# Reordering the first FFN group of a fused mLSTM and squared-ReLU FFN kernel on all its engine queues

## The chip, the cores and the metric

The kernel runs on one core of a Trainium2 chip. A core has five engines that work side by side, each with its own queue that is worked off strictly in the order of the program: TensorE (PE, the matmuls, with the loads of its weights shown as PEld), VectorE (DVE), ScalarE (ACT), GpSimd (POOL) and SyncE (SP), which here issues nearly all DMAs. Matmuls write to PSUM banks; the other data lies in SBUF. An instruction that needs another engine's result waits for a semaphore, and everything behind it on its own queue waits with it. The metric is the time of one execution on the device in microseconds (us), lower is better.

## The reference

The first part is an mLSTM cell over 4 batches, 8 heads, 768 time steps and heads of 40 columns, as a recurrence:

```python
for t in range(S):
    m_new = np.maximum(f_gate[:, :, t] + m, i_gate[:, :, t])
    f_stab = np.exp(f_gate[:, :, t] + m - m_new)
    i_stab = np.exp(i_gate[:, :, t] - m_new)
    m = m_new
    C = f_stab[:, :, None, None] * C + i_stab[:, :, None, None] * np.einsum('bhd,bhe->bhde', vt, kt)
    n = f_stab[:, :, None] * n + i_stab[:, :, None] * kt
    h_tilde = np.einsum('bhde,bhe->bhd', C, qt)
    nq = np.einsum('bhd,bhd->bh', n, qt)[:, :, None]
    denom = np.maximum(np.abs(nq), 1.0)
    o = 1.0 / (1.0 + np.exp(-o_gate[:, :, t]))
    y[:, :, t] = o * h_tilde / denom
```

Its output, as a matrix x of 3072 tokens by 320 columns, goes through an FFN with w_in (320 x 2048) and w_out (2048 x 320), whose values arrive as 64-bit floats:

```python
h = np.maximum(x @ w_in, 0.0)
return (h * h @ w_out).astype(np.float32)
```

## The kernel before, in words

The recurrence is computed by chunks of 128 tokens. There are 24 chunks, six to a batch; a chunk is called s. For each chunk these steps are written, each of them a small function:

- `load(s)`, `load_A(s)`, `load_o(s)` fetch k, q and v, the row of decays spread over the partitions, and the output gate. All are issued by SP.
- `weigh(s)`: POOL masks the decays (affine_select, L312), ACT makes the weights W from them (eight exponentials, L318), POOL multiplies v by the weights of the last row (vw, L329).
- `transposes(s)`: PE transposes k and q (L342); the copies out of PSUM are kT on ACT and qT on DVE (L346).
- `scores(s)`: PE multiplies qT and kT (L355). `weighted(s)`: DVE multiplies the scores by W into P_sb (L365).
- `attend(s)`: PE makes hi (the carried state times q, L376), dC (the state's increment, L383) and hp (P_sb times v, L390). DVE scales and adds them (num, L396 and L412; C_sb, L401), POOL updates the state (L404, L409), and DVE divides by the denominator and multiplies by the gate (dm and x_sb, L414 to L421). POOL copies the last 64 columns of x a second time (L422), so that PE can use both halves of its rows.
- `turn_rows(s)`: PE transposes x (L431), ACT copies it into xT (L432).

The FFN works on groups of four chunks (512 tokens). `ffn1` takes a pair of 128-column blocks of the hidden layer: six matmuls into two PSUM banks (L446, L451), the rectifier on ACT (r_sb, L454) and the square on DVE (g, L455). `ffn2` multiplies g by w_out (L493) in two parts for each chunk, and ACT copies the result out (L499). The first group is different: its chunks come out while it runs, so it is computed in two halves of 256 tokens with four units each by `ffn1_half` (L470, L477; rectifier L485, square L486). These eight units are called u0 to u7 here: u = 4 * half + the loop's own u.

The weights arrive as 64-bit floats and are rounded to 32 bits on the chip, in 26 pieces: ten of w_in (512 columns wide) and then sixteen of w_out (320 wide). One `rounding.step()` does one piece: two ACT operations of the piece after it (`words`, L179 and L181), three DVE operations (`join`, L190, L194, L195), one POOL add that writes the weights (L199), and a DMA that fetches the raw words of the fourth piece after it (L170). The pools bound how far these run ahead: four raw buffers, two of mag and low.

The order on every queue is written out by hand (`manual_schedule`): engines do not reorder, so the order of the statements is the order of the work. PSUM has eight banks: three for the attention ("at"), three for h_ps, two for o_ps; a pool hands its banks out in turn, and a writer waits until the readers of the tile that had the bank are done. `idle(n)` is n matmuls of zeros.

Before the loop over u, chunks 0 and 1 go through all their steps and chunk 2 through its transposes. Then a unit with an even u does score(s), turn_rows(s - 1), its rounding steps, ffn1_half, and the weights of chunk s + 1; one with an odd u does attend(s), its rounding steps, ffn1_half and transposes(s + 1). The number of rounding steps in u0 to u7 is 2, 3, 2, 4, 4, 4, 4 and 0. After the loop the general schedule runs four units of FFN to one chunk.

Of the kernel before, what the change touches and what calls it, by code (L numbers as in the profile page):

```python
# [9 lines left out]
F32 = mybir.dt.float32  # L10
# [19 lines left out]
def kernel(  # L30
# [326 lines left out]
                )  # L357
        d["sc"] = sc

    def weighted(s):  # L360
        d = st[s]
        sc = d["sc"]
        d["P"] = work.tile([P, 2, PR, P], F32, name="P_sb", bufs=1)
        for i in range(2):
            nc.vector.tensor_tensor(  # L365
                d["P"][:, i], sc[i], d["W"][:].rearrange("p (j two) t -> p j two t", two=2)[:, :, i, :], op=ALU.mult,
            )

    def attend(s):
        b, c = divmod(s, NB)  # L370
        d = st[s]
        C = st.get("C")
        if c > 0:
            hi = ps_at.tile([P, H, D1], F32, name="hi", tag="at")
            for j in range(PR):
                nc.tensor.matmul(  # L376
                    hi[:, 2 * j : 2 * j + 2, :].rearrange("p h d -> p (h d)"), lhsT=d["qT"][:, j, :],
                    rhs=C[:, j].rearrange("p h d -> p (h d)"), start=True, stop=True,
                )
        if c + 1 < NB:  # L380
            dC = ps_at.tile([P, PR, 2, D1], F32, name="dC", tag="at")
            for j in range(PR):
                nc.tensor.matmul(  # L383
                    dC[:, j].rearrange("p h d -> p (h d)"),
                    lhsT=d["kq"][:, 0, 2 * j : 2 * j + 2, :].rearrange("p h d -> p (h d)"),
                    rhs=d["vw"][:, 2 * j : 2 * j + 2, :].rearrange("p h d -> p (h d)"), start=True, stop=True,
                )
        hp = ps_at.tile([P, H, D1], F32, name="hp", tag="at")
        for h in range(H):
            nc.tensor.matmul(  # L390
                hp[:, h, :], lhsT=d["P"][:, h % 2, h // 2, :], rhs=d["va"][:, h, :], start=True, stop=True,
            )
        num = hp
        if c > 0:
            num = work.tile([P, H, D1], F32, name="num")
            nc.vector.tensor_tensor(  # L396
                num[:], hi[:], eA_T[:, b, c, :].unsqueeze(2).to_broadcast([P, H, D1]), op=ALU.mult,
            )
        if c + 1 < NB:
            Cn = work.tile([P, PR, 2, D1], F32, name="C_sb")  # L400
            nc.vector.tensor_tensor(Cn[:], dC[:], bdm[:], op=ALU.mult)  # L401
            if c > 0:
                Cd = work.tile([P, H, D1], F32, name="Cd")
                nc.gpsimd.tensor_tensor(  # L404
                    Cd[:], C[:].rearrange("p j i d -> p (j i) d"),
                    d["dec"][:].unsqueeze(2).to_broadcast([P, H, D1]), op=ALU.mult,
                )
                Cf = Cn[:].rearrange("p j i d -> p (j i) d")
                nc.gpsimd.tensor_tensor(Cf, Cf, Cd[:], op=ALU.add)  # L409
            st["C"] = Cn  # L410
        if c > 0:
            nc.vector.tensor_tensor(num[:], num[:], hp[:], op=ALU.add)  # L412
        dm = work.tile([P, H], F32, name="dm")
        nc.vector.tensor_scalar(dm[:], num[:, :, D], scalar1=-1.0, scalar2=1.0, op0=ALU.mult, op1=ALU.max)  # L414
        nc.vector.tensor_tensor(dm[:], dm[:], num[:, :, D], op=ALU.max)
        nc.vector.reciprocal(dm[:], dm[:])

        x = d["x"] = work.tile([P, 3 * P], F32, name="x_sb")
        x3 = x[:, :DM].rearrange("p (h d) -> p h d", d=D)
        nc.vector.tensor_tensor(x3, num[:, :, :D], d["og"], op=ALU.mult)  # L420
        nc.vector.tensor_tensor(x3, x3, dm[:].unsqueeze(2).to_broadcast([P, H, D]), op=ALU.mult)  # L421
        nc.gpsimd.tensor_copy(x[:, DM:], x[:, DM - KR : DM])  # L422

    def turn_rows(s):
        d = st[s]
# [31 lines left out]
    def ffn1_half(g, half, pp):  # L457
# [16 lines left out]
        for n in range(2):  # L474
            for i in range(2):
# [2 lines left out]
                    hs[i][:, n, :], lhsT=w_in2[rows, 2 * pp + n, :], rhs=xT[rows, 2, cols],  # L478
                    start=False, stop=(n == 1),
                )  # L480
        g4 = st["g2"][:, 4 * pp : 4 * pp + 4, cols].rearrange("p (n two) t -> p n two t", two=2)
        for i in range(2):
            r = ffn.tile([P, W], F32, name="r_sb", bufs=4)
            r2 = r[:].rearrange("p (n t) -> p n t", n=2)
            nc.scalar.activation(r2, hs[i][:], AF.Relu)  # L485
            nc.vector.tensor_tensor(g4[:, :, i, :], r2, r2, op=ALU.mult)  # L486

    def ffn2(g, j, part):
        if part == 0:
# [26 lines left out]
    def attend_on(s):  # L516
        do(attend, s)
        do(load, s + 4)
        if 4 <= s < 8:
            load_o(2 * s)  # L520
            load_o(2 * s + 1)
        elif 8 <= s < 16:
            load_o(s + 8)
# [72 lines left out]


    for half in range(2):
        for u in range(4):
            s = 2 * (half + 1) + u // 2  # L600
            if u % 2 == 0:
                score(s)
                if half or u:
                    turn_rows(s - 1)
            else:
                if u == 1:
                    for r in range(s, s + 2 + 2 * half):
                        sigmoid(r)
                attend_on(s)
            for _ in range(IN_DONE[min(u + 1, 3)] - rounding.done if half == 0 and u < 3 else 4):  # L610
                rounding.step()
            if half == 0 and u < 2:
                load(4 + u)
            ffn1_half(0, half, u)
            if u % 2 == 0:
                weigh_on(s + 1)
            else:
                transposes(s + 1)
            if half == 0:
                load_o(4 + u)  # L620
    assert rounding.done == len(pieces)
    turn_rows(5)


# [2 lines left out]
    for n in range(NPAIR, NU * NG):  # L627
        g, u = divmod(n, NU)
        s, at = GT + n // 4, n % 4
        if at == 0:  # L630
            do(score, s)
        if at == 1:
            attend_on(s)
        if at == 3:
            do(turn_rows, s)
            do(transposes, s + 1)
            if s in (7, 15):
                for r in range(s + 1, s + 9):
# [37 lines left out]
```

## Time and profile before

| | before |
|---|---|
| median of 3 runs (lowest to highest) | 636.58 us (636.46 to 636.78) |
| the profiled execution | 636.74 us |
| its span | 635.0 us |
| PE busy | 598.2 us, 94% of the span |
| DVE busy | 226.9 us, 36% |
| ACT busy | 193.2 us, 30% |
| POOL busy | 100.8 us, 16% |
| mean granted TensorE clock | 0.968 |
| moved by DMA | 42.47 MB, mean 67 GB/s |

The profile is one execution. Its span is the time from the first to the last instruction, which is 1.74 us shorter than the execution. A line of a group names the source line, the engine, the operation, out <- in, the count, the busy time and the mean duration in ns. In the chain of waits each row has a start, a duration and what the end of the program waited for then. The granted clock is the share of full speed at which TensorE was run. Some matmuls appear as two records, so counts of L470 or L493 are twice those in the code.

### The profile page before, as it was taken

To read this page: it belongs to the slowest core of one execution; us is meant where nothing else is said; L and a number is where in the kernel's file an instruction comes from. 1 tells how busy PE (TensorE), PEld (TensorE's weight loads), DVE (VectorE), ACT (ScalarE), POOL (GpSimd) and SP (SyncE) were. 2 spreads that over 40 slices of the span, in tenths; PEclk is the share of its full clock that TensorE was granted. 3 is DMA by queue.
4 is the path that set the end of the run, shared out by engine and by line. 5 is a ranking of instruction groups with operands and counts; after the bars stand their busy time and mean duration, and the time that the engine had idled before them with its cause. 6 is when DMAs were issued, how large, how long until landed. Compare 5 with 4: busy or idle time off the path is not lost.

```text
span 635.0 us, 7569 instructions
## 1 busy us (share of the span) xinstructions
PE 598.2 (94%) x2877; PEld 392.9 (62%) x2877; DVE 226.9 (36%) x444; ACT 193.2 (30%) x476; POOL 100.8 (16%) x137
## 2 busy tenths in 40 slices
PE   9974949599999999999999999999999999999997
PEld 5753837477764557764567764567764567743575
DVE  7657667751213432222431223431223431212200
ACT  4646536342153232123132144232114132012200
POOL 3334324221101201001102101001201110000000
PEclk9978878699999999999999999999999999999999
DMA  9889466455312314313313312313211000000000
GB/s 195 207 184 193 85 150 146 105 86 96 63 54 42 74 34 85 63 45 65 52 33 86 63 43 33 64 42 76 44 45 34 0 1 15 17 10 2 0 22 21
DMA packets 130900, 42.47 MB, mean 67 GB/s; under 512 B 101072, under 2 KB 127696, under 8 KB 130864
## 3 DMA queue, kind: packets, MB, share of 16 engines
q1 hardware_dynamic: 130768, 41.79, 31.6%
q8 instruction: 23, 0.38, 0.2%
q10 hardware_dynamic: 96, 0.20, 0.1%
q14 instruction: 13, 0.11, 0.1%
HBM read 37.95 MB, written 4.03 MB: 66 GB/s over the span
## 4 chain that ended last, share of the span: by engine, by line
PE 87%; DVE 5%; ACT 3%; DMA 2%; issue 1%; POOL 1%; SPq 0%; POOLq 0%; ACTq 0%; DVEq 0%
PE o_ps L493 33%; PE h_ps L446 22%; PE h_ps L451 7%; PE hp L390 6%; PE tp L355 5%; PE h_ps L470 3%; PE tp L342 3%; PE hi L376 3%; PE dC L383 2%; PE tp L431 2%; DMA raw<-in_moe_w_out_dram 1%; DVE mag L194 1%; ACT W_sb L318 1%; DVE g L486 1%; DMA kq<-in_q_dram 1%
## 5 line engine op out<-in xcount | busy, mean ns | idle before, releaser
L493 PE MATMUL o_ps<-w_out,g 128*128 128x320 f32 x768 | 213.8, 435 | 0.0
L493 PEld LDWEIGHTS o_ps<-w_out,g 128*128 128x128 f32 x768 | 143.5, 190 | 57.9 <-issue 0.8
L446 PE MATMUL h_ps<-xT,w_in 128*128 128x512 f32 x320 | 146.9, 602 | 0.0
L455 DVE TENSOR_TENSOR g<-r_sb 128x512 f32<-128x512 f32 x80 | 51.7, 688 | 153.2 <-ACT r_sb L454 153.2
L446 PEld LDWEIGHTS h_ps<-xT,w_in 128*128 128x128 f32 x320 | 57.7, 190 | 69.9 <-issue 65.2
L454 ACT ACTIVATE r_sb<-h_ps 128x512 f32<-128x512 f32 x80 | 43.5, 595 | 162.6 <-PE h_ps L451 162.5
L499 ACT COPY y_sb<-o_ps 128x320 f32<-128x320 f32 x24 | 10.2, 425 | 190.4 <-PE o_ps L493 190.4
L355 PE MATMUL tp<-qT,kT 40*128 40x128 f32 x384 | 30.9, 307 | 30.1 <-DVE qT L346 26.3
L318 ACT ACTIVATE W_sb<-A_bc,b_T 128x128 f32<-128x128 f32 x176 | 53.7, 391 | 5.1 <-POOL A_bc L312 5.1
L355 PEld LDWEIGHTS tp<-qT,kT 40*128 40x128 f32 x384 | 27.2, 210 | 40.1 <-issue 31.4
L365 DVE TENSOR_TENSOR P_sb<-tp,W_sb 128x512 f32<-128x512 f32 x48 | 30.9, 684 | 57.3 <-PE tp L355 57.3
L390 PE MATMUL hp<-va,P_sb 128*128 128x41 f32 x384 | 46.1, 280 | 0.0
L451 PE MATMUL h_ps<-xT,w_in 64*128 64x512 f32 x160 | 45.2, 641 | 0.0
L390 PEld LDWEIGHTS hp<-va,P_sb 128*128 128x128 f32 x384 | 44.9, 192 | 0.1
L346 DVE COPY qT<-tp 128x512 f32<-128x512 f32 x23 | 15.8, 687 | 73.6 <-PE tp L342 73.6
L470 PE MATMUL h_ps<-xT,w_in 128*128 128x256 f32 x128 | 36.8, 451 | 0.6 <-ACT xT L432 0.6
L409 POOL TENSOR_TENSOR C_sb<-C_sb,Cd 128x328 f32<-128x328 f32 x16 | 14.0, 876 | 138.8 <-DVE C_sb L401 138.6
L470 PEld LDWEIGHTS h_ps<-xT,w_in 128*128 128x128 f32 x128 | 29.0, 233 | 6.3 <-ACT xT L432 1.0
L329 POOL TENSOR_TENSOR vw<-va,W_sb 128x328 f32<-128x328 f32 x20 | 15.0, 749 | 112.0 <-ACT W_sb L318 107.2
L451 PEld LDWEIGHTS h_ps<-xT,w_in 64*128 64x128 f32 x160 | 12.0, 184 | 30.3 <-issue 30.3
L422 POOL COPY x_sb<-x_sb 128x64 f32<-128x64 f32 x24 | 5.9, 244 | 139.3 <-DVE x_sb L421 139.3
L342 PE MATMUL tp<-ident,kq 128*128 128x128 f32 x192 | 25.4, 274 | 0.2 <-DMA kq<-in_q_dram 0.2
(79 smaller groups left out, 472.1 us busy)
## 6 DMA issues: line engine op xcount, KB each, us to landing
A_bc<-a_rows SPq DMA_DIRECT2D x22, 512.0 KB, 3.8
raw<-in_moe_w_out_dram SPq DMA_DIRECT2D x16, 320.0 KB, 3.4
raw<-in_moe_w_in_dram SPq DMA_DIRECT2D x8, 512.0 KB, 4.9
kq<-in_k_dram SPq DMA_DIRECT2D x24, 160.0 KB, 4.0
kq<-in_q_dram SPq DMA_DIRECT2D x24, 160.0 KB, 4.5
va<-in_v_dram SPq DMA_DIRECT2D x24, 160.0 KB, 4.0
og<-in_o_gate_dram SPq DMA_DIRECT2D x24, 160.0 KB, 4.0
out_dram<-y_sb SPq DMA_DIRECT2D x24, 160.0 KB, 1.8
```

The lines of the kernel that those rows point to most:

```text
L318: nc.scalar.activation(d["W"][:, i * n + h, :], A[i][:, h, :], AF.Exp, bias=b_T[:, b, c, i * n + h : i * n + h + 1],)
L342: nc.tensor.transpose(tp[:, j, :], d["kq"][:, i, 2 * j : 2 * j + 2, :].rearrange("p h d -> p (h d)"), ident[:],)
L355: nc.tensor.matmul(sc[i][:, j, :], lhsT=d["kT"][rows, j, :], rhs=d["qT"][rows, j, :], start=True, stop=True,)
L365: nc.vector.tensor_tensor(d["P"][:, i], sc[i], d["W"][:].rearrange("p (j two) t -> p j two t", two=2)[:, :, i, :], op=ALU.mult,)
L376: nc.tensor.matmul(hi[:, 2 * j : 2 * j + 2, :].rearrange("p h d -> p (h d)"), lhsT=d["qT"][:, j, :], rhs=C[:, j].rearrange("p h d -> p (h ...
L390: nc.tensor.matmul(hp[:, h, :], lhsT=d["P"][:, h % 2, h // 2, :], rhs=d["va"][:, h, :], start=True, stop=True,)
L446: nc.tensor.matmul(h[:], lhsT=w_in[:, a, fb * P : (fb + 1) * P], rhs=xT[:, a, :], start=(a == 0), stop=False,)
L451: nc.tensor.matmul(hs[i][:], lhsT=w_in2[rows, p, :], rhs=xT[rows, 2, :], start=False, stop=True)
L454: nc.scalar.activation(r[:], hs[i][:], AF.Relu)
L455: nc.vector.tensor_tensor(st["g2"][:, 2 * p + i, :], r[:], r[:], op=ALU.mult)
L470: nc.tensor.matmul(hs[i][:, n, :], lhsT=w_in[:, a, fb * P : (fb + 1) * P], rhs=xT[:, a, cols], start=(n == 0 and a == 0), stop=False,)
L493: nc.tensor.matmul(o_ps, lhsT=st["g2"][:, fb, j * P : (j + 1) * P], rhs=w_out[:, fb, :], start=(fb == 0), stop=(fb == NF - 1),)
```

## The change: the same instructions in another order

The computation stays the same, and so does the number of matmuls of the FFN and the attention. What changes:

- `weighted` writes two tiles instead of one with two parts. Chunk 1 takes its two from the pool of r_sb (four buffers), the others from P_sb with two buffers.
- `attend` ends after the matmuls and the state; what makes x of it is a function of its own, `normalise`. The copy of x's last columns moves from POOL to DVE.
- `ffn1_half` issues the matmuls alone. `relu_half` (ACT) and `square_half` (DVE) are called later: the rectifiers of a unit at the start of the next unit, the squares towards that unit's end.
- Ahead of the loop, scores of chunks 0 and 1 are weighted together, two groups of idle matmuls (six and four) go, the rounding steps stand between the attends, and transposes(2) stand between the two remaining groups of idle matmuls.
- In the loop, u0 puts its half unit ahead of scores(2). In odd units the transposes of the next chunk stand ahead of the half unit.
- The rounding steps are spread out: one near the start of each unit and the others at its end, up to the counts in NEXT (6, 8, 10, 12, 15, 18, 21, 24 pieces done after u0 to u7; four are done ahead of the loop). The last two pieces are done after the loop, behind the first W2 unit.
- The fetches of k, q and v of chunks 4 to 9 are spread over the odd units as 4; 5, 6; 7, 8; 9.

```diff
-    def weighted(s):
+    def weighted(s, spare=False):
...
-        d["P"] = work.tile([P, 2, PR, P], F32, name="P_sb", bufs=1)
+        d["P"] = []
         for i in range(2):
+            t = ffn.tile([P, W], F32, name="r_sb", bufs=4) if spare else work.tile([P, W], F32, name="P_sb")
...
-        if c > 0:
-            nc.vector.tensor_tensor(num[:], num[:], hp[:], op=ALU.add)
+
+    def normalise(s):
+        d = st[s]
+        num = d["num"]
+        if num is not d["hp"]:
+            nc.vector.tensor_tensor(num[:], num[:], d["hp"][:], op=ALU.add)
...
-        nc.gpsimd.tensor_copy(x[:, DM:], x[:, DM - KR : DM])
+        nc.vector.tensor_copy(x[:, DM:], x[:, DM - KR : DM])
...
-        g4 = st["g2"][:, 4 * pp : 4 * pp + 4, cols].rearrange("p (n two) t -> p n two t", two=2)
-        for i in range(2):
-            r = ffn.tile([P, W], F32, name="r_sb", bufs=4)
-            r2 = r[:].rearrange("p (n t) -> p n t", n=2)
-            nc.scalar.activation(r2, hs[i][:], AF.Relu)
-            nc.vector.tensor_tensor(g4[:, :, i, :], r2, r2, op=ALU.mult)
+        st["half"] = hs, st["g2"][:, 4 * pp : 4 * pp + 4, cols].rearrange("p (n two) t -> p n two t", two=2)
+
+    def relu_half():
+        if "half" in st:
+            hs, g4 = st.pop("half")
+            rs = []
+            for h in hs:
+                rs.append(ffn.tile([P, 2, W // 2], F32, name="r_sb", bufs=4))
+                nc.scalar.activation(rs[-1][:], h[:], AF.Relu)
+            st["relu"] = rs, g4
+
+    def square_half():
+        if "relu" in st:
+            rs, g4 = st.pop("relu")
+            for i, r in enumerate(rs):
+                nc.vector.tensor_tensor(g4[:, :, i, :], r[:], r[:], op=ALU.mult)
...
     def attend_on(s):
         do(attend, s)
+        do(normalise, s)
...
-    rounding.step()
     weighted(0)
-    idle(6)
+    weighted(1, spare=True)
     load(2)
     load_A(2)
     sigmoid(0)
     sigmoid(1)
     attend(0)
-    weighted(1)
     rounding.step()
+    normalise(0)
     load_o(2)
     load_o(3)
+    attend(1)
+    normalise(1)
+    rounding.step()
     load(3)
     load_A(3)
-    idle(4)
-    attend(1)
     turn_rows(0)
     idle(4)
+    transposes(2)
+    idle(4)
+    turn_rows(1)
+    rounding.step()
     weigh_on(2)
-    transposes(2)
-    turn_rows(1)
-
-
-    for half in range(2):
-        for u in range(4):
-            s = 2 * (half + 1) + u // 2
-            if u % 2 == 0:
-                score(s)
-                if half or u:
-                    turn_rows(s - 1)
+
+
+    NEXT = (6, 8, 10, 12, 15, 18, 21, 24)
+    for u in range(8):
+        s = 2 + u // 2
+        relu_half()
+        if u % 2 == 0:
+            if u == 0:
+                ffn1_half(0, 0, 0)
+                scores(s)
             else:
-                if u == 1:
-                    for r in range(s, s + 2 + 2 * half):
-                        sigmoid(r)
-                attend_on(s)
-            for _ in range(IN_DONE[min(u + 1, 3)] - rounding.done if half == 0 and u < 3 else 4):
-                rounding.step()
-            if half == 0 and u < 2:
-                load(4 + u)
-            ffn1_half(0, half, u)
-            if u % 2 == 0:
-                weigh_on(s + 1)
-            else:
-                transposes(s + 1)
-            if half == 0:
-                load_o(4 + u)
-    assert rounding.done == len(pieces)
+                scores(s)
+                turn_rows(s - 1)
+                ffn1_half(0, u // 4, u % 4)
+            rounding.step()
+            weighted(s)
+            weigh_on(s + 1)
+            square_half()
+        else:
+            if u in (1, 5):
+                for r in range(s, s + 2 + u // 2):
+                    sigmoid(r)
+            attend(s)
+            rounding.step()
+            normalise(s)
+            transposes(s + 1)
+            ffn1_half(0, u // 4, u % 4)
+            square_half()
+            for r in {1: (4,), 3: (5, 6), 5: (7, 8), 7: (9,)}[u]:
+                load(r)
+            if u > 4:
+                load_o(2 * s)
+                load_o(2 * s + 1)
+        while rounding.done < NEXT[u]:
+            rounding.step()
+        if u < 4:
+            load_o(4 + u)
+    relu_half()
+    square_half()
     turn_rows(5)
...
             ffn2(g, *divmod(u - NPAIR, 2))
+        while rounding.done < len(pieces):
+            rounding.step()
         if at == 2:
```

More of the change, by code (lines that the diff above doesn't have):

```diff
@@ L358, in scores @@
         d["sc"] = sc
-    def weighted(s):
+    def weighted(s, spare=False):
         d = st[s]
-        sc = d["sc"]
-        d["P"] = work.tile([P, 2, PR, P], F32, name="P_sb", bufs=1)
+        d["P"] = []
         for i in range(2):
+            t = ffn.tile([P, W], F32, name="r_sb", bufs=4) if spare else work.tile([P, W], F32, name="P_sb")
+            t = t[:].rearrange("p (j t) -> p j t", j=PR)
+            d["P"].append(t)
             nc.vector.tensor_tensor(
-                d["P"][:, i], sc[i], d["W"][:].rearrange("p (j two) t -> p j two t", two=2)[:, :, i, :], op=ALU.mult,
+                t, d["sc"][i], d["W"][:].rearrange("p (j two) t -> p j two t", two=2)[:, :, i, :], op=ALU.mult,
             )
@@ L387, in attend @@
                 )
-        hp = ps_at.tile([P, H, D1], F32, name="hp", tag="at")
+        hp = d["hp"] = ps_at.tile([P, H, D1], F32, name="hp", tag="at")
         for h in range(H):
             nc.tensor.matmul(
-                hp[:, h, :], lhsT=d["P"][:, h % 2, h // 2, :], rhs=d["va"][:, h, :], start=True, stop=True,
+                hp[:, h, :], lhsT=d["P"][h % 2][:, h // 2, :], rhs=d["va"][:, h, :], start=True, stop=True,
             )
-        num = hp
+        d["num"] = hp
         if c > 0:
-            num = work.tile([P, H, D1], F32, name="num")
+            num = d["num"] = work.tile([P, H, D1], F32, name="num")
             nc.vector.tensor_tensor(
```

## The prediction

> **What bounds the kernel now.** I read the granted clock and the busy time by stretch first, then who waits for whom, then the chain of waits through one pair of units. A chunk is 128 tokens (number s); u0 to u7 are the eight half-width units of the first FFN group.
>
> ```profile
> PEclk9978878699999999999999999999999999999999
> ```
> ```profile
> 20.50:138.33 117.83, 85.80 (x521) 70.65 (x520) 79.63 (x148) 60.04 (x136) 43.74 (x49) 0.83 0.66 139
> 63.15:90.30 27.15, 18.35 (x108) 15.27 (x108) 18.54 (x33) 12.26 (x28) 10.04 (x11) 0.81 0.66 139
> 138.33:635.00 496.67, 493.25 (x2240) 310.55 (x2238) 131.52 (x268) 122.63 (x312) 51.14 (x73) 1.00 0.21 43
> ```
> The columns are the stretch, its length, busy PE, PEld, DVE, ACT and POOL, the granted clock, the DMA share and GB/s. From 138.33 us on, PE is busy for 493.25 of 496.67 us at clock 1.00: the change can't shorten that. Before it, from 20.50 to 138.33, PE works 85.80 of 117.83 us, at a mean clock of 0.83. A pair of units (second row) takes 27.15 us.
>
> ```profile
> PE tp L355 <- DVE qT L346: 26.3, 4, 8.8
> ```
> ```profile
> 37.13 2.08 PE L355 MATMUL tp<-qT,kT 40*128 40x128 f32 x16 [3.76 <-ACT kT L346]
> ...
> 137.24 1.16 PE L355 MATMUL tp<-qT,kT 40*128 40x128 f32 x16 [1.35 <-DVE qT L346]
> ```
> The largest wait of PE is the scores waiting for the copy of qT by DVE: 26.3 us in four places. After a pause of 3.76 us the same 16 matmuls take 2.08 us, after 1.35 us 1.16: long pauses also cost clock. The chain through the second of the long pauses shows why the copy is late:
>
> ```profile
> 82.16 4.64 DMA raw<-in_moe_w_out_dram
> ...
> 86.88 0.49 ACT mag L179
> ...
> 87.74 0.49 ACT r_sb L485
> 88.25 1.29 DVE g L486 x2
> 89.55 0.61 DVE qT L346
> ...
> 90.30 2.08 PE tp L355 x16
> ...
> 93.24 0.49 ACT xT L432
> 93.78 6.73 PE h_ps L470 x16
> ```
> A rounding step waits for its raw weights, the rectifiers stand behind it on ACT, the squares behind those on DVE, and the copy of qT behind the squares. PE has nothing in its queue but the scores that need this copy.
>
> **The change, part by part.** First the floor: PE's work from the end of scores(1) to the first W2 matmul, each kind at its full-clock duration.
>
> ```profile
> 6.75 0.86 PE idle L532 x4
> ...
> 19.41 1.09 PE tp L355 x16
> ...
> 21.90 0.85 PE dC L383 x8
> 22.76 1.77 PE hp L390 x16
> ...
> 126.08 1.06 PE h_ps L477 x8
> 127.14 1.05 PE hi L376 x8
> ...
> 129.94 3.53 PE h_ps L470 x16
> ...
> 138.40 4.50 PE o_ps L493 x16
> ...
> 177.50 0.33 PE tp L431 x3
> 177.82 0.87 PE tp L342 x8
> ```
> Scores(1) end at 19.41 + 1.09 = 20.50. Then come attend(0), 0.85 + 1.77 = 2.62; attend(1) to (4), each 1.05 + 0.85 + 1.77 = 3.67, together 14.68; attend(5), which makes no dC, 2.82; five scores, 5.45; eight half units of 3.53 + 1.06 = 4.59, 36.72; five times transposes, 4.35; six turn_rows, 1.98; two idle groups left, 1.72 (the groups of six and four ahead of the attends go). Sum 70.34: the first W2 matmul could start at 90.8 instead of 138.40. So 47.6 us is the most that can be won.
>
> What the edits do to PE's order: transposes(s+1) now stand ahead of a half unit, so 4.59 us of matmuls cover the copies of kT and qT; in u0 the half unit is put ahead of scores(2). The rectifiers move to the start of the next unit and the squares behind the qT copy, so that copy waits for neither. Cover that could fail: three banks hold the half unit's results and two are used per unit, so the second tile of a unit waits for the first rectifier of the unit before, which stands first in ACT's unit. P_sb in separate tiles lets weighted(1) run while attend(0) is still ahead. The copy of x's last 64 columns goes from POOL to DVE: six small instructions, which I put at 0.2 us each (not shown on DVE; between 0 and the 0.49 of the 320-column x operations), and POOL's select and adds no longer wait behind it.
>
> Next the waits that remain. I walked the four in-order queues by hand with these rows:
>
> ```profile
> 66.44 0.42 DVE L190 TENSOR_SCALAR mag<-mag 128x512 f32<-128x512 f32 x1
> 66.89 0.43 DVE L194 TENSOR_SCALAR mag<-mag 128x512 int32<-128x512 int32 x1
> ...
> 67.96 0.42 DVE L190 TENSOR_SCALAR mag<-mag 128x512 f32<-128x512 f32 x1
> 68.42 1.37 DVE L194 TENSOR_SCALAR mag<-mag 128x512 int32<-128x512 int32 x1
> ```
> ```profile
> 36.59 0.74 POOL L329 TENSOR_TENSOR vw<-va,W_sb 128x328 f32<-128x328 f32 x1 [2.56 <-ACT W_sb L318]
> ...
> 68.19 1.31 POOL L199 TENSOR_TENSOR w_in<-mag,low 128x512 int32<-128x512 int32 x1 [6.94 <-DVE mag L195]
> ```
> ```profile
> 34.06 2.44 ACT L318 ACTIVATE W_sb<-A_bc,b_T 128x128 f32<-128x128 f32 x8 [2.49 <-POOL A_bc L312]
> ...
> 50.17 1.28 ACT L275 ACT_TABLE_LOAD   x1
> 51.46 0.83 ACT L275 ACTIVATE og<-og 128x320 f32<-128x320 f32 x2
> ```
> ```profile
> L312 POOL TENSOR_SCALAR_AFFINE_SELECT A_bc<-A_bc 128x1024 f32<-128x1024 f32 x5 | 6.4, 1278 | 0.0
> ```
> A rounding step of 512 columns holds DVE for 1.52 us (66.44 to 67.96), or 0.94 more where L194 falls on POOL's add (1.37 for 0.43). An add is 1.31 on POOL, a select 1.28, the eight exponentials 2.44, vw 0.74. The words of a 320-column step take ACT 87.74 - 86.88 = 0.86; I put those of 512 at 1.2, an estimate between 0.86 and 1.38 (by columns).
>
> - u0, turn_rows(1): the first half unit waits for the xT copy, 0.49 and latency: 0.6.
> - u0 to u1: dC(2) needs vw(2). hp(1) ends near 26.8; normalise 2.2, a step 1.5, qT 0.6 and a step slowed by POOL 2.5 bring DVE to 33.7; add, select, exponentials and vw to 39.5. PE would be there at 30.7 + 4.59 + 1.09 + 1.05 = 37.4: 2.1.
> - u1 to u2: scores(3) need kT(3). ACT holds, behind the exponentials of chunk 3 (ending near 44.7), two words (2.4), two rectifiers (1.0), the sigmoids with their table load (2.1) and kT (0.6), so 50.8. The wait of transposes(3) for C_sb's product, the second tile's for the rectifier and this one: 2.8 together.
> - u3: transposes(4) behind num(3), and w_in's last piece from POOL: 0.8.
> - u4: turn_rows(3) stands just ahead of the half unit that reads it, with two rectifiers before the copy on ACT: 0.7.
> - u6 to u7: transposes(6) need the bank of hi(5), which num(5) frees; DVE is behind three rounding steps and their words: 2.2.
>
> Together 9.2; all else lies beside PE. For the clock after these pauses (none of them over 2.2 us, and 1.35 us cost nothing visible above) and for DVE operations that meet POOL where I had them free I add 2.5, between 0 and the 9.9 us of rival A. The first W2 matmul then starts at 90.8 + 9.2 + 2.5 = 102.5, 35.9 us earlier.
>
> L194 is also where a rule speaks against the change.
>
> ```profile
> L194 DVE TENSOR_SCALAR mag<-mag 128x320 int32<-128x320 int32 x16 | 12.8, 802 | 0.5
> L194 DVE TENSOR_SCALAR mag<-mag 128x512 int32<-128x512 int32 x8 | 7.2, 898 | 0.3
> ```
> Against 0.43 for 512 columns (so about 0.3 for 320), these 24 lose 16 x 0.5 + 8 x 0.47, some 12 us, to POOL. My sum takes half of that as gone, since a step stands apart from the one before it in most units. The Trainium skill, "SBUF — State Buffer", section "SBUF: two separate sides", says that VectorE and GpSimd take a shared port pair by an exclusive lock and the loser blocks for the whole instruction. The row of 68.42 agrees: L194 ends 0.3 us after the add. By that rule spreading the steps frees DVE only if POOL is idle at those moments, and it will be busier; that is rival A.
>
> The rest: two W2 steps go behind the first W2 unit. Pieces 24 and 25 are the last that ffn2's second part reads; P(6), two slowed steps and the add need some 6 us of DVE and POOL, covered by 4.50 + 2.62 and the first six of its eight matmuls, 3.4. Without that cover they would cost up to 6 us. Loads: chunks 5 and 7 are fetched two units later, two units (8 us of PE work or more) ahead of their transposes, against 4.64 us of the raw wait; SP's queue is in order, so a fetch behind load_A waits for the exponentials, but raw weights are fetched four steps ahead.
>
> The profiled execution took 636.74 (span 635.0, 1.74 around it), 0.16 above the median: 636.58 - 35.9 = 600.7, say 601.
>
> **The rivals.**
>
> A. DVE becomes the bound. If contention stays as it is, DVE has the 79.63 us of the first stretch, plus the step that moves behind 20.50 (2.1) and the copies (1.2), less the two steps that leave (3.0): 79.9, from 20.6, so 100.5 with no idle moment. My walk has it idle for 9.5 us besides (for hp(1), scores(2), words). 110 for the first W2 matmul: 608. For it: L194's rows. Against: the squares now follow PSUM operations, not adds.
>
> B. Transfers become the bound.
>
> ```profile
> DMA packets 24097, 8.17 MB, mean 182 GB/s; under 512 B 18758, under 2 KB 23366, under 8 KB 24094
> ```
> That is 20 to 65 us, with DMA busy nearly throughout. My order issues about 12.1 MB between 44 and 101 us (raw 5.8, k, q and v 3.0, A 2.1, o 1.3), 212 GB/s. At 182 it takes 66.5 us, to 110.5: 609. Against: some 3 MB of it is for chunks 7 and later and can be late.
>
> C. Pauses overlap and PE is nearly the bound: 3 us of waits in place of 11.7, so 592.
>
> D. Slower. ACT's order puts each unit's rectifiers behind the words of the last step, which wait for POOL's add two steps before. If PE's second tile waits for them in every unit, the gain of 47.6 is used up at 5.9 us in each of eight. At pauses of 4 us, each followed by cold scores (2.08 for 1.09, +1.0) and a cold half unit (6.73 for 3.53, half of it taken, +1.6), that point is passed: 8 x 6.6 = 53 us, 642. Against: it needs every rectifier late, and the raw wait behind this pause goes with the bursts of four steps.
>
> E. Nothing changes: the copies of qT stay the last to come, behind the steps instead of the squares, and the pairs keep 27 us: 636. For it speaks only that DVE does the same work.
>
> **How the numbers follow.** The forecast (597 to 605) gets 0.46, A 0.20, B 0.10, C 0.16, D 0.06, E 0.02. The prediction is that of the first, 601. Down to 590 lie C and the floor (636.6 - 47.6 = 589.0), up to 614 A and B with another 5 us; D and E and a little beyond each are left out. Faster by over 0.2% (1.3 us, about what a measurement of this kernel can tell from no change): 0.92; within it 0.02; slower 0.06.
>
> **What would show it.** First W2 matmul near 102 us; the granted clock at 0.9 or more from 40 us on; PE's wait for qT at under 3 us in total, and new PE waits of about 2 us for vw, kT and num. L194's mean well under 0.8 us would confirm the spreading, an unchanged one rival A; a landing time of raw weights above 6 us with ACT waiting for it, B. The prediction is wrong if any pause of PE above 3.5 us stands between u0 and u7, or if the stretch behind the first W2 matmul is no longer 497 us.

## The result, and the profile after

| | before | changed |
|---|---|---|
| median (lowest to highest) | 636.52 us (634.66 to 636.78, 4 runs) | 608.4 us (607.17 to 609.54, 4 runs) |
| ratio to before, 95% interval | | 0.9564 [0.9538, 0.959] |
| span of the profiled execution | 635.0 us | 606.7 us |
| first W2 matmul at | 138.33 us | 110.03 us |

The change makes the kernel 28 us faster. That is the direction forecast and within the range up to 614, but 7 us short of the 601 predicted and outside the 597 to 605 of the main forecast; it is the time that rival A gave, 608. The page's first line and its row of the granted clock:

```profile
span 606.7 us, 7558 instructions
...
PEclk9988998999999999999999999999999999999999
```

The busy times by stretch (length, then PE, PEld, DVE, ACT, POOL, granted clock, DMA share, GB/s):

```profile
21.33:110.03 88.70, 78.93 (x515) 66.45 (x514) 80.34 (x149) 56.73 (x130) 40.48 (x40) 0.92 0.90 188
...
110.03:606.70 496.67, 493.25 (x2240) 310.55 (x2238) 145.48 (x295) 125.43 (x319) 49.55 (x58) 1.00 0.20 43
```

The second stretch is the same 496.67 us as before: nothing was gained or lost behind the first W2 matmul. All of it lies in the first, from the end of scores(1) on, which fell from 117.83 to 88.70 us; 0.8 of these 29.1 us is lost again because scores(1) ended later in this execution. In it DVE is now busy for 80.34 us, 91%; before it did 79.63 us of work in the longer stretch. Nearly the same work (two of the squares now fall behind the first W2 matmul), no cheaper, packed closely.

Who waits for whom, from 20 to 112 us (us in total, times, longest):

```profile
DVE mag L190 <- ACT mag L179: 3.8, 4, 1.4
...
PE tp L342 <- DVE num L398: 3.3, 3, 2.1
...
PE dC L385 <- POOL vw L329: 2.7, 1, 2.7
...
PE h_ps L476 <- ACT r_sb L495: 1.2, 1, 1.2
...
PE tp L355 <- DVE qT L346: 0.8, 2, 0.4
```

PE's 26.3 us of waiting for qT are 0.8. New are a pause for vw(2) and waits for num in front of the transposes. PE's own timeline shows what follows the two longest pauses:

```profile
41.04 1.91 PE L385 MATMUL dC<-vw,kq 128*128 128x82 f32 x8 [2.65 <-POOL vw L329]
42.74 3.55 PE L392 MATMUL hp<-va,P_sb 128*128 128x41 f32 x16
46.09 1.95 PE L342 MATMUL tp<-ident,kq 128*128 128x128 f32 x8
47.83 5.39 PE L476 MATMUL h_ps<-xT,w_in 128*128 128x256 f32 x16
...
55.49 3.62 PE L476 MATMUL h_ps<-xT,w_in 128*128 128x256 f32 x16
...
71.17 1.16 PE L355 MATMUL tp<-qT,kT 40*128 40x128 f32 x16 [0.41 <-DVE qT L346]
...
93.25 1.99 PE L476 MATMUL h_ps<-xT,w_in 128*128 128x256 f32 x8 [1.25 <-ACT r_sb L495]
...
101.67 0.66 PE L342 MATMUL tp<-ident,kq 128*128 128x128 f32 x4 [2.10 <-DVE num L398]
102.17 5.31 PE L476 MATMUL h_ps<-xT,w_in 128*128 128x256 f32 x16
```

After 2.65 us the matmuls of u1 run at about half speed (granted clock 0.50 from 43 to 51 us) until partway through the half unit, whose first part takes 5.39 us for the 3.62 of u2. After 2.10 us the half unit of u7 takes 5.31. After 0.41 and 1.25 us the matmuls keep their speed.

The chain of waits through this stretch shows which engine they hang on. These are pieces of it:

```profile
87.89 0.60 DVE qT L346
88.49 1.20 DVE g L502 x2
...
95.20 1.10 POOL A_bc L312
96.33 1.46 ACT W_sb L318 x5
...
101.21 0.42 DVE num L398
...
102.33 5.14 PE h_ps L476 x16
```

Added up by engine, the chain runs over DVE for 37.0 of the 88.70 us, PE for 27.6, ACT for 8.3 and POOL for 7.3; before it ran over PE for 46.9 of 117.83 us, DVE for 30.3, ACT for 17.4 and transfers for 8.6. A profile infers such a chain from semaphores, so it is a pointer that the experiments have to confirm. The slow half unit of u7 lies on it too, so its 1.7 us seem to be a real cost of PE's clock.

The last view is DVE's groups in the first stretch (busy us, mean ns of one):

```profile
L502 DVE TENSOR_TENSOR g<-r_sb 128x512 f32<-128x512 f32 x14 | 11.8, 886 | 0.0
L194 DVE TENSOR_SCALAR mag<-mag 128x320 int32<-128x320 int32 x14 | 8.8, 631 | 0.5
...
L194 DVE TENSOR_SCALAR mag<-mag 128x512 int32<-128x512 int32 x9 | 7.5, 829 | 0.3
L195 DVE SCALAR_TENSOR_TENSOR mag<-raw,mag 128x512 int32<-128x512 int32 x9 | 7.4, 823 | 0.3
L190 DVE TENSOR_SCALAR mag<-mag 128x512 f32<-128x512 f32 x9 | 5.5, 611 | 1.4 <-ACT mag L179 1.4
...
L421 DVE TENSOR_TENSOR dm<-dm,num 128x8 f32<-128x8 f32 x5 | 2.5, 501 | 0.2
```

L194 fell from 802 to 631 ns and from 898 to 829, but L195 rose from 692 to 823, L190 from 419 to 611, the squares from 834 to 886, and an operation on eight columns (L421) from 271 to 501. So DVE's loss seems moved, not removed; that it is a loss to POOL is what experiment 4 tests.

### The profile page after: what moved, and what is told of

It reads as the page before. It is cut to its first block, busy times and chain, and to the rows that moved or that the text cites. A ratio compares the mean times of both kernels' runs of the same rounds, so it can differ in the third digit from the quotient of the medians.

```text
span 606.7 us, 7558 instructions
## 1 busy us (share of the span) xinstructions
PE 592.3 (98%) x2870; PEld 389.3 (64%) x2871; DVE 239.6 (39%) x468; ACT 192.4 (32%) x476; POOL 95.9 (16%) x113
## 4 chain that ended last, share of the span: by engine, by line
PE 89%; DVE 6%; ACT 2%; issue 1%; POOL 1%; POOLq 0%; DVEq 0%; ACTq 0%
PE o_ps L509 35%; PE h_ps L452 23%; PE h_ps L457 7%; PE hp L392 6%; PE tp L355 3%; PE tp L342 3%; PE dC L385 3%; PE hi L378 2%; PE h_ps L476 2%; PE tp L437 1%; DVE mag L194 1%; DVE mag L195 1%; ACT W_sb L318 1%; PE idle L549 1%; POOL A_bc L312 1%
## 5 line engine op out<-in xcount | busy, mean ns | idle before, releaser
L452 PEld LDWEIGHTS h_ps<-xT,w_in 128*128 128x128 f32 x320 | 57.7, 190 | 69.9 <-issue 65.2
L367 DVE TENSOR_TENSOR P_sb<-tp,W_sb 128x512 f32<-128x512 f32 x46 | 29.6, 684 | 45.1 <-PE tp L355 43.0
L346 DVE COPY qT<-tp 128x512 f32<-128x512 f32 x23 | 15.8, 687 | 70.2 <-PE tp L342 70.2
L476 PE MATMUL h_ps<-xT,w_in 128*128 128x256 f32 x128 | 33.1, 415 | 3.0 <-ACT r_sb L495 1.2
L457 PEld LDWEIGHTS h_ps<-xT,w_in 64*128 64x128 f32 x160 | 12.0, 184 | 30.3 <-issue 30.3
L476 PEld LDWEIGHTS h_ps<-xT,w_in 128*128 128x128 f32 x128 | 26.1, 210 | 8.1 <-ACT r_sb L495 1.6
L355 PEld LDWEIGHTS tp<-qT,kT 40*128 40x128 f32 x384 | 24.1, 187 | 10.8 <-issue 6.8
L355 PE MATMUL tp<-qT,kT 40*128 40x128 f32 x384 | 27.1, 280 | 0.8 <-DVE qT L346 0.8
L342 PEld LDWEIGHTS tp<-ident,kq 128*128 128x128 f32 x192 | 23.0, 147 | 4.5 <-DVE num L398 3.8
```

What stands on the lines that cost most here:

```text
L342: nc.tensor.transpose(tp[:, j, :], d["kq"][:, i, 2 * j : 2 * j + 2, :].rearrange("p h d -> p (h d)"), ident[:],)
L355: nc.tensor.matmul(sc[i][:, j, :], lhsT=d["kT"][rows, j, :], rhs=d["qT"][rows, j, :], start=True, stop=True,)
L367: nc.vector.tensor_tensor(t, d["sc"][i], d["W"][:].rearrange("p (j two) t -> p j two t", two=2)[:, :, i, :], op=ALU.mult,)
L452: nc.tensor.matmul(h[:], lhsT=w_in[:, a, fb * P : (fb + 1) * P], rhs=xT[:, a, :], start=(a == 0), stop=False,)
L457: nc.tensor.matmul(hs[i][:], lhsT=w_in2[rows, p, :], rhs=xT[rows, 2, :], start=False, stop=True)
L476: nc.tensor.matmul(hs[i][:, n, :], lhsT=w_in[:, a, fb * P : (fb + 1) * P], rhs=xT[:, a, cols], start=(n == 0 and a == 0), stop=False,)
```

## The experiments

Two theories stood against each other. P: the missing 7 us are PE's pauses with the half clock behind them. D, rival A: DVE is the bound, and PE's pauses only show where it is late. Each run was compared with the kernel before on the same chip; where I give a difference to the changed kernel, it is that of the two ratios, times 636.5 us.

**1. The pause filled** (x1_warm): `warm(12)` issues twelve matmuls of zeros into a free bank of o_ps; the function itself is left out below.

```diff
+        if s == 2:
+            warm(12)
         if c + 1 < NB:
             dC = ps_at.tile([P, PR, 2, D1], F32, name="dC", tag="at")
```

> The changed kernel with twelve idle matmuls in u1, between hi(2) and dC(2), where PE pauses 2.65 us. Theory P (the shortfall against 601 us is TensorE's clock after pauses of 2.1 and 2.65 us): dC, hp, transposes and the half unit of u1 return from 1.91 + 3.34 + 1.75 + 5.18 to about 0.85 + 1.77 + 0.87 + 3.53 us, and the first W2 matmul comes 3 to 5 us earlier, 603.5 to 605.5 us. Theory D (DVE is the bound, rival A): these matmuls get faster all the same, but scores(3) then wait for qT, whose copy ended at 53.6 us, and the time stays within 0.8 us of 608.4. If the matmuls stay slow, their duration is not the clock's.

608.05 us, ratio 0.9572 [0.9548, 0.9596]: no gain. PE's timeline of this run:

```profile
37.33 2.75 PE L556 MATMUL idle<-zeros 128*128 128x512 bf16 x12
40.14 1.12 PE L387 MATMUL dC<-vw,kq 128*128 128x82 f32 x8
41.10 1.92 PE L394 MATMUL hp<-va,P_sb 128*128 128x41 f32 x16
...
44.94 3.85 PE L478 MATMUL h_ps<-xT,w_in 128*128 128x256 f32 x16
...
52.88 2.08 PE L355 MATMUL tp<-qT,kT 40*128 40x128 f32 x16 [3.02 <-DVE qT L346]
...
55.58 5.28 PE L478 MATMUL h_ps<-xT,w_in 128*128 128x256 f32 x16
...
82.28 1.48 PE L342 MATMUL tp<-ident,kq 128*128 128x128 f32 x8 [0.80 <-DVE num L400]
83.55 4.96 PE L478 MATMUL h_ps<-xT,w_in 128*128 128x256 f32 x16
```

The slow matmuls were the clock: dC, hp and the half unit are back at full speed. But PE then stands 3.02 us in front of scores(3) until DVE has copied qT, and is cold one unit later, and again at 83 us. Some 5 us won on PE came back whole. The matmuls that are slow now stand behind waits for DVE, so this is theory D's case; of this run's chain DVE has 44.0 us and PE 20.4.

**2. A rounding step put behind POOL's select** (x3_select_first): the fourth rounding step goes behind the weights of chunk 2, which should take away the cause of that pause.

```diff
-    rounding.step()
     weigh_on(2)
+    rounding.step()
```

> The changed kernel with the fourth rounding step behind the weights of chunk 2 instead of ahead of them, so that POOL's select and ACT's exponentials no longer stand behind that step. Theory P: vw(2) comes some 2.5 us earlier, the pause of 2.65 us before dC(2) goes and with it the half clock behind it: 5 to 8 us, 600.5 to 603.5 us. Theory D: only the 1.7 us go for which DVE waited for W(2): 1 to 2 us, 606.5 to 607.5.

607.93 us, ratio 0.9568 [0.9547, 0.959]: no gain, a little less than D gave. The exponentials of chunk 2 start 2.1 us earlier, but the step behind them now makes DVE wait for its words, and dC waits for P_sb instead of vw:

```profile
42.09 1.97 PE L385 MATMUL dC<-vw,kq 128*128 128x82 f32 x8 [2.90 <-DVE P_sb L367]
```

The pause was not taken away (2.90 us for 2.65, with slow matmuls behind it), so this run does not decide between the theories. It shows only that PE met a late DVE there by another route.

**3. Work taken from DVE** (x2_noclamp): the clamp of each rounding step, L190, is left out.

```diff
-            nc.vector.tensor_scalar(
-                mag, mag, scalar1=word_as_float(0x38000000), scalar2=word_as_float(0x47EFFFFF),
-                op0=ALU.max, op1=ALU.min,
-            )
```

> The changed kernel without the first of the three DVE operations of each rounding step (the clamp of the magnitude, L190; it is left out for all 26 pieces). DVE is busy with it for 10.9 us between 21.33 and 110.03 us. Theory D: the first W2 matmul comes 7 to 11 us earlier, 597.5 to 601.5 us. Theory P: PE's pauses get a little shorter and their cold clock stays: 1 to 3 us earlier, 605.5 to 607.5.

602.72 us, ratio 0.9482 [0.9464, 0.9501], 5.2 us faster than the changed kernel: more than P allows, less than D alone. The stretch up to the first W2 matmul and the wait of DVE (the clamp gone, L190 is the shift in this kernel):

```profile
20.78:103.69 82.91, 76.30 (x517) 65.11 (x515) 68.58 (x126) 56.69 (x129) 40.41 (x40) 0.94 0.89 198
```
```profile
DVE mag L190 <- ACT mag L179: 8.1, 4, 4.0
```

DVE lost 11.8 us of work, the stretch only 5.8. DVE's waits for the words of ACT rose from 3.8 to 8.1 us. But the chain of waits no longer runs mainly over DVE: PE has 49.6 of its 82.9 us and DVE 6.6. With DVE relieved, PE is the bound again, busy for 92% of the stretch, and its remaining waits for other engines and its slow matmuls set the time.

**4. POOL's share of DVE's time** (x4_noadd): the third DVE operation writes the weights itself and POOL's add goes; the weights are cut off instead of rounded.

```diff
-            nc.vector.tensor_scalar(bits, bits, scalar1=3, scalar2=None, op0=ALU.logical_shift_left)
+            nc.vector.tensor_scalar(bits, bits, scalar1=3, scalar2=0x3FFFFFFF,
+                                    op0=ALU.logical_shift_left, op1=ALU.bitwise_and)
...
-                bits, in0=self.raws[n][:, :w, 1], scalar=-0x80000000, in1=bits,
+                dst.bitcast(I32), in0=self.raws[n][:, :w, 1], scalar=-0x80000000, in1=bits,
...
-            nc.gpsimd.tensor_tensor(dst.bitcast(I32), bits, low.bitcast(I32), op=ALU.add)
```

> The changed kernel without POOL's add in the rounding steps: the third DVE operation writes the weights itself, so they are cut off instead of rounded; the number of DVE operations is the same. It asks what DVE loses to POOL. L194 has means of 829 ns (512 columns) and 631 (320) against 430 and 330 where POOL rests, and L190, L195 and the squares are stretched too, some 16 us in all. Theory D with contention as the cause: 8 to 12 us earlier, 596.5 to 600.5 us, and these means fall to their lowest values. Theory P: up to 2 us (the wait for w_in's last piece, 0.6, and a little).

601.32 us, ratio 0.9461 [0.944, 0.9482], 6.6 us faster than the changed kernel.

```profile
21.15:103.32 82.17, 74.94 (x517) 63.11 (x515) 68.40 (x151) 58.58 (x135) 17.73 (x19) 0.96 1.00 204
```
```profile
L194 DVE TENSOR_SCALAR mag<-mag 128x320 int32<-128x320 int32 x14 | 5.8, 414 | 0.5
...
L194 DVE TENSOR_SCALAR mag<-mag 128x512 int32<-128x512 int32 x9 | 4.7, 519 | 0.3
```

With the same operations DVE is busy for 68.40 us instead of 80.34, though two squares more fall in this stretch: at least 12 us of its time in the changed kernel are lost to POOL's adds inside its own instructions, where a profile shows them as busy. L194 did not fall to its lowest values, 330 and 430 ns; POOL still works for 17.73 us here. Of the 12 us the time got back 6.6, less than the 8 to 12 that D gave and more than the 2 that P allowed. Part of the rest is PE again (52.4 of the chain's 82.2 us; DVE has 13.3), and ACT's words are late here too. Without the add the words also stop waiting for POOL, so the 6.6 us are not the price of the contention alone; the 12 us of DVE's busy time are. The Trainium skill, "SBUF — State Buffer", section "SBUF: two separate sides", describes a mechanism that fits: a port pair that one of the two engines has to itself for a whole instruction. The rows agree: operations with an operand in PSUM keep their duration (P_sb has a mean of 683 ns with the adds and without).

**5. The parts of the change undone one at a time.** (y1_relu_in_place) Rectifiers and squares right behind their half unit (shown for odd units; even ones and u0 alike, with both calls):

```diff
             ffn1_half(0, u // 4, u % 4)
+            relu_half()
             square_half()
```

> The changed kernel with one part undone: the rectifiers and squares stand right behind their half unit again. On DVE the squares then stand ahead of what follows in the unit and wait for matmuls that have only just been issued. Theory D: DVE is held some 2 to 4 us in each of eight units, and since it has no slack this goes into the time: 15 to 30 us later, 623 to 638 us. Theory P: PE keeps its covers and only its pauses grow: 2 to 8 us later, 610 to 616 us.

627.83 us, ratio 0.9878 [0.9856, 0.9901]. DVE stands in front of the squares:

```profile
DVE g L502 <- ACT r_sb L495: 24.5, 8, 5.6
```

(y2_bursts) All steps of a unit at the place of its first, in even and odd units (the loop at a unit's end goes):

```diff
-            rounding.step()
+            while rounding.done < NEXT[u]:
+                rounding.step()
```

> The changed kernel with all rounding steps of a unit where its first one stands, two or three in a row, with the same counts per unit. Theory D: more of L194 meets POOL's add again (9 more steps follow another directly, 0.6 to 0.9 us each), and normalise and the qT copy come later: 5 to 10 us later, 613 to 618 us. Theory P: the qT copies get later by a step or two in odd units, 3 to 6 us.

616.65 us, ratio 0.97 [0.9683, 0.9718]. PE's waits for qT are back, 2.80 and 2.24 us the longest, with cold matmuls behind them:

```profile
75.35 2.08 PE L355 MATMUL tp<-qT,kT 40*128 40x128 f32 x16 [2.80 <-DVE qT L346]
...
78.83 6.67 PE L476 MATMUL h_ps<-xT,w_in 128*128 128x256 f32 x16 [0.57 <-ACT xT L438]
```

PE's longest pause is another, 5.8 us of dC for P_sb. The reason given for this run was only half right: L194's means are lower here than in the changed kernel (579 ns at 320 columns). What the rows show instead is DVE late with P_sb and qT, and its waits for words, 11.3 us.

(y3_transposes_behind) The transposes behind the half unit:

```diff
-            transposes(s + 1)
             ffn1_half(0, u // 4, u % 4)
+            transposes(s + 1)
             square_half()
```

> The changed kernel with the transposes of odd units behind the half unit again, so that no matmuls cover the copies of kT and qT; the squares stay behind the qT copy. In each of four pairs PE waits for the two copies with an empty queue, at least 0.87 + 0.6 us and the semaphores. Theory D: DVE, which reaches the qT copy late in any case, loses up to 1 us per pair: 2 to 6 us later, 610 to 614. Theory P: four pauses of 2 to 4 us with cold matmuls behind them, 12 to 20 us later, 620 to 628.

612.61 us, ratio 0.9639 [0.9619, 0.9659].

Against 0.9564 the three parts are worth 20.0, 8.7 and 4.8 us, all three within what D gave and none within P's ranges (the spread steps cost more than P's 6 us). They sum to more than the 28 us of the whole, so they are not independent. Of the three, the late rectifiers and squares are worth most and the transposes ahead least. The other parts (the order ahead of the loop and in u0, the two P_sb tiles, the moved fetches) were not undone alone.

**6. Work moved from DVE to ACT** (x5_square_act).

```diff
-                nc.vector.tensor_tensor(g4[:, :, i, :], r[:], r[:], op=ALU.mult)
+                if i == 0:
+                    nc.vector.tensor_tensor(g4[:, :, i, :], r[:], r[:], op=ALU.mult)
+                else:
+                    nc.scalar.activation(g4[:, :, i, :], r[:], AF.Square)
```

> The changed kernel with the second of the two squares of each half unit on ACT instead of DVE (eight operations of 0.9 us each leave DVE; ACT gets eight of about 0.5 us and is busy for 57 of 89 us so far). Theory D: 3 to 6 us earlier, 602.5 to 605.5 us. Theory P: no gain or up to 2 us later, as words and kT copies stand behind more on ACT.

607.78 us, ratio 0.9565 [0.9548, 0.9583]: no gain. Here D alone fails; the number is P's, and so is the reason that P gave, words late on ACT, though TensorE's clock has no part in it. DVE's busy time up to this run's first W2 matmul and its wait for words:

```profile
21.33:110.75 89.42, 79.02 (x516) 66.43 (x515) 75.63 (x142) 60.83 (x139) 40.60 (x40) 0.92 0.92 187
```
```profile
DVE mag L190 <- ACT mag L179: 9.2, 4, 3.4
```

4.7 us less work, 5.4 us more waiting. The chain stays with DVE (38.8 us) and ACT (15.8); PE has 8.4. A rounding step is a ring: ACT's words for one piece wait until POOL's add has freed the buffers of an earlier one, DVE's join waits for words, POOL for the join, and the words stand in ACT's queue behind exponentials and sigmoids. Theory L, argued from these waits: DVE and ACT bound each other through this ring.

**7. The ring loosened** (x9_words_ahead, then with the square: x10_ahead_square, then with qT on ACT and the select first: x11_all). The edit of x9_words_ahead; `low` gets three buffers too, and `num` and `Cd` one each.

```diff
-            mag = conv.tile([P, 512], F32, name="mag")
+            mag = conv.tile([P, 512], F32, name="mag", bufs=3)
...
-                if len(self.a) == len(self.b):
-                    self.words()
-                self.words()
+                while len(self.a) < min(len(self.b) + 3, len(pieces)):
+                    self.words()
```

> The changed kernel with the words of a rounding step on ACT one step earlier (three buffers of mag and low in place of two; room made by one buffer of num and of Cd, each used by one engine alone). DVE's waits for these words, 3.8 us in the changed kernel, should go. Theory D with DVE alone as the bound: 2 to 4 us earlier, 604.5 to 606.5 us. Theory L (DVE and ACT bound each other in a loop of words, join and POOL's add): the same here. If words on ACT now stand ahead of kT copies and rectifiers that PE waits for: 0 to 3 us later.

608.12 us, ratio 0.9562 [0.9548, 0.9575]: no gain, where D and L gave 2 to 4 us. DVE's waits for words only fell to 2.9 us. The third case came: PE's banks wait for rectifiers, which stand behind words that now wait for raw weights:

```profile
ACT mag L179 <- DMA raw<-in_moe_w_out_dram: 8.1, 4, 3.7
...
PE h_ps L475 <- ACT r_sb L494: 4.3, 2, 3.1
```

> The kernel before this one with the second square of each half unit on ACT as well. Moved alone, the square took 5.3 us of work from DVE and gave back 5.4 us as waits for ACT's words, and the time stayed. Theory L: with the words a step ahead the wait doesn't come back, and the time falls by 4 to 7 us against 608.4, to 601.5 to 604.5 us. If DVE's work isn't what bounds these units, it stays within 1 us of the words-ahead kernel alone.

605.71 us, ratio 0.9525 [0.9509, 0.954], 2.5 us faster than the changed kernel: the square now pays, but half of what L gave.

> The kernel before this one with the copies of qT of chunks 1 to 6 on ACT too, and the fourth rounding step behind the weights of chunk 2. DVE loses another 3 us of copies and 1.7 us of waiting for W(2). Theory L: DVE has 72 us of work left in the stretch, ACT some 63, and PE 70 at full clock: 598 to 602 us. Against: kT and qT are copied one after the other by the engine that also has the words, so that PE waits for the pair longer; then no better than 603.

605.01 us, ratio 0.9517 [0.9504, 0.953], short of L's 598 to 602. L's number has now failed three times, so the ring is a part of the limit and not the whole. The rows name what took over, the transfers:

```profile
ACT mag L179 <- DMA raw<-in_moe_w_out_dram: 9.4, 5, 4.9
```
```profile
44.00:107.00 63.00, 51.66 (x348) 42.24 (x348) 48.73 (x96) 47.45 (x110) 28.53 (x30) 0.97 0.94 195
```

**8. Transfers out of the way** (x12_loads_late), on top of x11_all.

```diff
-            for r in {1: (4,), 3: (5, 6), 5: (7, 8), 7: (9,)}[u]:
+            for r in {1: (4,), 3: (5,), 5: (6,), 7: (7,)}[u]:
                 load(r)
-            if u > 4:
-                load_o(2 * s)
-                load_o(2 * s + 1)
...
     turn_rows(5)
+    load(8)
+    load(9)
+    for r in range(8, 12):
+        load_o(r)
```

> The kernel before this one (words ahead, squares and qT copies shared with ACT, select first) with transfers that nobody in these units needs taken out of them: k, q and v of chunks 8 and 9 and o of 8 to 11 (1.6 MB of the 12.3 moved between 44 and 107 us) are fetched behind the loop, those of chunks 6 and 7 two units later. With DVE relieved, ACT waited 11.6 us for raw weights, DMA being busy for 94% of that stretch. Theory T (transfers are the next bound): these waits fall to under 5 us and the time by 2 to 5 us, to 600 to 603 us. Theory L alone (queues of DVE, ACT and PE): within 1 us of 605.0, and the wait moves to the rectifiers and words.

600.11 us (599.57 to 603.07), ratio 0.945 [0.9427, 0.9473]: 7.3 us below the changed kernel and in the range of theory T. It is the fastest of the runs, with x4_noadd, whose weights are not rounded, inside its interval. ACT's waits for raw weights, 9.4 us for w_out and 2.2 for w_in in x11_all, fell to 3.4 and 1.2, and the DMA share from 0.94 to 0.82:

```profile
ACT mag L179 <- DMA raw<-in_moe_w_out_dram: 3.4, 3, 2.4
...
ACT mag L179 <- DMA raw<-in_moe_w_in_dram: 1.2, 1, 1.2
```
```profile
44.00:102.00 58.00, 52.29 (x351) 43.42 (x350) 49.55 (x98) 47.93 (x111) 28.29 (x30) 0.94 0.82 189
```

Its first W2 matmul is at 101.72 us. Two causes are mixed here: the raw transfers themselves (21.9 us of the chain in x11_all, 15.7 here) and their place in SP's queue behind other fetches (5.2 and 0.8); these runs do not separate them. Which of its parts could be left out was not tried, nor the later loads without the others.

## Why the prediction was right, and where it was off

- **The floor and what lies behind it**: right. The stretch behind the first W2 matmul is the same 496.67 us, and no pause of PE reached 3.5 us.
- **The pauses**: ten of 9.7 us in total for the 9.2 predicted, the main ones at the places named: vw(2) 2.65 (2.1), num(5) 2.10 (2.2), xT twice 0.57 (0.6 and 0.7). That the totals agree so closely is luck in part. The wait of scores(3) (part of 2.8) is missing, because the slow half unit before it covered it: in x1_warm, where that half unit is fast, it is 3.02 us, and for qT. In its place stand 1.25 us for a rectifier in u6 and 0.81 for num(4).
- **The allowance of 2.5 us for clock and contention**: the step that failed. In its place stand 10.0 us (110.03 - 90.8 - 9.2). Scores(1) ended 0.8 us later in this execution; matmuls at half clock take 5.2 us more in u1 and 1.7 in u7, though I had taken pauses up to 2.2 us as nearly free of that; the other 2 are pauses and gaps of a few tenths. But experiment 1 shows that the 5.2 us were not the cause: paid or not, the time is the same, because DVE sets the pace there. The forecast's own terms said so: rival A's sum with half of L194's 12 us taken off, 20.6 + 73.9 + 9.5, puts the first W2 matmul at 104, later than the 102.5 forecast. I added up PE's pauses and did not hold the sum against DVE's.
- **Rival A** was the mechanism in the main. It had 79.9 us of DVE's work and 9.5 of idling, the first W2 matmul at 110 and 608 us; measured were 80.34 and 8.4, 110.03 and 608.4. The work was reasoned; that the idling fits is luck in part, for of the places named only the words show (3.8 us); 1.7 are for W(2), and most of the rest is in gaps. I gave A 0.20 because the squares now follow operations on PSUM. They did, and still their mean rose to 886 ns: the pairs behind a qT copy took 1.28 us, those behind P_sb 2.09 to 2.34, with an add or a select of POOL beside them. What matters is not which DVE operation goes before, but whether POOL is working, and POOL has nearly the same work (40.48 us after 43.74) in three quarters of the time. My "half of the 12 us goes" was for L194 alone. Against 0.43 and 0.3 us it still loses some 8, so a third went, and the other operations took that over: experiment 4 finds 12 us lost to POOL's adds in the changed kernel.
- **The signs**: PE's wait for qT (0.8 us) and the new waits came as said. The first W2 matmul at 102 and a clock of 0.9 from 40 us on did not: it is 0.85 between 46 and 64 us. L194's mean under 0.8 us at 320 columns would have confirmed the spreading against rival A; it fell to 631 ns and A came true all the same. A sign has to be taken from DVE's whole busy time, not from one of its operations.
- A alone is not the whole: taking 5 to 12 us from DVE gave 0 to 6.6 us back. In experiments 3 and 4 PE then has most of the chain, in experiment 6 ACT's words are late. How the limit is shared between the ring of the rounding steps, PE and the transfers stays open.
- **Rival B** did not happen here (no row has ACT waiting for raw weights), but DMA is busy for 90% of the stretch, and in x11_all and x12_loads_late the transfers cost time.
- **The two W2 steps behind the loop and the load of each moved fetch** cost nothing that a row shows.

## What to carry to other kernels

When a reordering closes an engine's pauses, add up each other engine's busy time over the shortened stretch before trusting the sum of remaining pauses: here DVE, busy for 91% of it, set the pace, and its busy time hid waits for another engine that packing did not remove. Filling a pause of PE was then worth nothing; test this by giving the other engine less to do, and look at the chain again, which here went back to PE. And look at the ring behind it: work moved away came back as waits, and paid only once the queue that feeds it ran ahead and the transfers not needed yet were out of the way.

## What the runs showed of the hardware that I had not expected

- TensorE's clock fell after pauses of 2.65 and 2.10 us (half unit 5.39 and 5.31 us for 3.62), not after 1.25. The Trainium skill, "TensorE: Matmul & The Clock Gate", section "What's actually happening", puts the fall behind an idle window of about 3.4 us; the measured pauses are shorter, so here shorter ones are already at risk. No length of a pause divides the cases: in x2_noclamp a pause of 1.56 us was followed by slow matmuls and one of 1.84 us was not, and in x1_warm one of 0.80 us was (granted clock 0.50 from 84 to 86 us, half unit 4.96). What else decides is not shown.
- DVE's small operations can lose as much beside POOL as its large ones. This is L421, which has eight columns, in the changed kernel, and the POOL add beside the slow one, which ends 0.03 us before it:

```profile
29.06 0.17 DVE L421 TENSOR_TENSOR dm<-dm,num 128x8 f32<-128x8 f32 x1
...
50.48 1.20 DVE L421 TENSOR_TENSOR dm<-dm,num 128x8 f32<-128x8 f32 x1
```
```profile
50.37 1.28 POOL L199 TENSOR_TENSOR w_in<-mag,low 128x512 int32<-128x512 int32 x1
```
